# Top-k attention and a SmeLU MLP: transposes of the unit matrix in TensorE's program until the MLP's first products

## The chip, the cores and the metric

The kernel runs on one core of a Trainium2 chip. The metric is the device time of one execution in microseconds (us), of which the median over several executions is compared. Five engines work side by side: TensorE (PE; its weight loads are shown apart as PEld), VectorE (DVE), ScalarE (ACT), GpSimd (POOL) and SyncE (SP), which issues the transfers. Each runs its own list of instructions in order and waits for the others at semaphores.

## What is computed

```python
# q, k, v: (8 batches, 8 heads, 576 rows, 64); float32 throughout
scores = q @ k.T / sqrt(64)
kth    = 32nd largest score of each row
attn   = softmax(where(scores >= kth, scores, -1e9))
x      = (attn @ v), heads side by side        # (4608, 512)
h      = x @ w_in                              # (4608, 2048)
g      = where(h >= 1, h, where(h <= -1, 0, (h + 1)**2 / 4))
out    = g @ w_out                             # (4608, 512)
```

## The kernel before, in words

**Steps.** A step is one block of 128 query rows for a pair of heads. `rounds` lists (batch, block t), and each block has four head pairs (`hp`), so that the first four steps, m = 0 to 3, are block 0 of batch 0. In a step TensorE makes the scores (`sp`, L354), ACT scales them into `s` (L355), DVE finds the 32nd largest with MAX8 and MATCH_REPLACE8 (L368 to L447) and masks the exponentials `e` (L454), which ACT made (L391). Then the masked weights are turned: in the early steps by TensorE, as a product with a diagonal matrix that also divides by the row sum (`diag` on ACT, L404; `pw`, L469, and `pwt`, L475; copied by ACT to `wT`, L472 and L476). TensorE multiplies them with the values (`po`, L502), and ACT copies the result to `xT` (L515). When four head pairs of a block are there, `mlp` puts the block's products (`ph`, L535, and `py`, L558) into the list `pending`.

**The order of work.** Inside `run` the order of PE, DVE, ACT and POOL is the program's (`tc.manual_schedule`); SP's is the scheduler's. The loop over m has seven places (`SLOTS`) per step. Each place issues a part of DVE's search for step m, and certain places issue the rest: place 1 turns the weights of step m - 1 (`transpose_w`), place 2 multiplies those by the values (`values_until`), place 4 makes the scores of step m + 2 (`begin_at`), place 6 the queries of step m + 3. In the first steps (`early`) the 32 pieces of the two weight matrices are converted as well, four to a step, with ACT (L146, L147), DVE (L155) and POOL (L157). At the end of a place `advance` takes products from `pending` as far as a budget allows; `spent` counts what has been taken. `pending` is empty until `values_until` has done step 3, which is in place 2 of m = 4.

**Before the loop.** Once, while the first keys are being loaded, TensorE transposes the unit matrix 20 times (`warm`, L672). `ident` is 128x128 float32, made by POOL. Then come keys (`pk`, `pkt`), queries (`pq`) and the scores of steps 0 and 1.

**PSUM** holds 8 banks: tag `a` two buffers of two banks (`sp`, `pw`, `pwt`, `pk`, `pq`), tag `ph` three of one bank (`ph`, `po`), and tag `py` one bank, first used by the MLP's second product.

Of the kernel before, what the change touches and what calls it, by code (L numbers as in the profile page):

```python
# [11 lines left out]
F32 = mybir.dt.float32  # L12
# [14 lines left out]
def kernel(  # L27
# [10 lines left out]
    nc = tc.nc  # L38
# [3 lines left out]
    P = 128  # L42
# [4 lines left out]
    NT = S // P  # L47
# [13 lines left out]
    ident = const.tile([P, P], F32, name="ident")  # L61
# [64 lines left out]
    def load(pool, i, bufs=3, parts=1):  # L126
        if i < n_pieces * parts and i not in loaded:
            if room:
                loaded[i] = room[i % len(room)]
            else:  # L130
                loaded[i] = pool.tile([P, 2 * WC // parts], U32, name="raw", bufs=min(bufs, 2))
            c = i % parts * (WC // parts)
            nc.sync.dma_start(out=loaded[i], in_=pieces_of_weights[i // parts][1][:, c:c + WC // parts].bitcast(U32))
# [42 lines left out]
    def run(ctx, paired):  # L176
# [5 lines left out]
        ps = ctx.enter_context(tc.tile_pool(name="ps", bufs=1, space=PSUM))  # L182
# [103 lines left out]
        def finish_turns():  # L286
            while turns:
                turns.pop(0)()
# [174 lines left out]
        def transpose_w(st):  # L463
            w = st["e"]
            st["wT"] = wT = (late or words).tile([P, BLOCKS, P], F32, name="wT", bufs=4 if late else 1)
            pt = ps.tile([P, 2, NT, P], F32, name="pw", tag="a", bufs=2)
            for i in range(2):
                for c in range(NT):
                    nc.tensor.matmul(pt[:, i, c, :], w[:, i, main(i)][:, c * P:(c + 1) * P], st["rz"][:, i, :],  # L469
                                     start=True, stop=True)  # L470
            for i in range(2):
                nc.scalar.copy(wT[:, i * (NT + 1):i * (NT + 1) + NT], pt[:, i])  # L472
            pt = ps.tile([P, P], F32, name="pwt", tag="a", bufs=2)
            for i in range(2):
                nc.tensor.matmul(pt[i * TL:(i + 1) * TL, :], w[:, i, tail(i)], st["rz"][:, i, :], start=True, stop=True)  # L475
            nc.scalar.copy(wT[:, NT], pt)  # L476
# [123 lines left out]
        pending = deque()  # L600
        total, spent = len(chunks) * (NK * NF + NF * DM // P), 0
# [4 lines left out]
        def convert(time):  # L606

            nonlocal converted, begun
            while begun < min(converted + (2 if paired else 1), n_pieces):
                pipe.append(convert_piece(words, begun, not paired))  # L610
                next(pipe[-1])
                begun += 1
            next(pipe.popleft())
            converted += 1
            usable[converted] = time
            for i in range(begun, converted + (len(room) or 2)):
                load(words, i)

        def inspect():
            nonlocal inspected  # L620
            if paired and inspected < 2 * n_pieces:
                inspect_piece(late, inspected)
                inspected += 1
# [7 lines left out]
        def take():  # L631

            nonlocal spent, due, pe_time, taken
            cost, pieces, work, _ = pending[0]
            if pieces > converted or usable[pieces] > pe_time + 0.5:
                return False
            pending.popleft()
            due -= cost
            spent += cost
            pe_time += cost * UNIT_TIME  # L640
            work()
            taken = work.func
            return True

        def advance(amount, until):

            nonlocal due, pe_time
            due = due + amount if pending else 0.0
            pe_time = max(pe_time, until - 4.0)
            while pending and due >= pending[0][0] and pe_time < until and take():  # L650
                pass
            due = min(due, 24.0)
# [84 lines left out]
        for m in range(n + 2):  # L737
            early = converted < n_pieces
            if not early and first_late is None:
                first_late = m  # L740
            elif not early and late is None:
                conversion.close()
                room.clear()
                late = ctx.enter_context(tc.tile_pool(name="late", bufs=1))

            share, left = (total - spent) / (n + 2 - m), sum(x[0] for x in pending)
            for r in sorted(ready):
                if r + 4 > m and r >= valued:
                    share = min(share, left / (r + 4 - m))
                    left += NK * NF + NF * DM // P  # L750
            top_k, parts = None, [0] * SLOTS
            if m < n:
                top_k = weights(state[m], state[m - 1] if m > 0 else None, state[m + 1] if m + 1 < n else None)
                parts = [1] * SLOTS if early else [1, 1, 0, 1, 1, 1, 1]
                start = max(dve_time, scored[m])
                now_converting = range(0, SLOTS, 2)
                dve_time = start + K_TIME + PIECE_TIME * min(len(now_converting), n_pieces - converted)
                done[m] = dve_time
                state[m]["by_tensor"] = early or m >= n - 2
            for slot in range(SLOTS):  # L760
                now = start + (dve_time - start) * (slot + 1) / SLOTS
                for _ in range(parts[slot]):
                    next(top_k, None)
                if m < n and converted < n_pieces:
                    if slot in now_converting:
                        convert(now)
                elif slot == 3 and late is not None:
                    if m % 2:
                        inspect()
                    elif paired:  # L770
                        load(late, inspected, 1, 2)
                if slot == 1 and 1 <= m <= n and state[m - 1]["by_tensor"]:
                    pe_time = max(pe_time, done[m - 1] + 2.0) + 1.0
                    transpose_w(state[m - 1])
                    ready_at[m - 1] = pe_time + 1.8
                if slot == 3 and 1 <= m <= n and state[m - 1] is not None and not state[m - 1]["by_tensor"]:
                    move_w(state[m - 1])
                    ready_at[m - 1] = done[m - 1] + 15.0
                if slot == 3:
                    finish_turns()  # L780
                if slot == 2 and m == n and paired:
                    judge(ps, att)
                if slot == 2 and (early or m == first_late or m >= n - 1):
                    values_until(m)
                if m == 0 and slot in (1, 2):
                    next(first)
                if slot == 2 and not early:
                    if m % 2 == 0:
                        while pending and taken is not None and taken.__name__ == "hidden" and take():
                            pass  # L790
                    values_until((m - 2) // 2 * 2)
                if slot == (4 if early else 2):
                    begin_at(m + 2)
                if slot == (6 if early else 1):
                    queries(m + 3)
                    if (m < n and prep is None and next_keys < B and steps[m][0] == next_keys - 1 and steps[m][1] >= 1
                            and (next_keys > 1 or converted == n_pieces)):
                        prep = (turned_keys_of if next_keys > 1 else keys_of)(next_keys)
                    if prep is not None and (m % 2 == 0 or next_keys == 1):
                        got = next(prep, None)  # L800
                        pe_time += 0.5 if next_keys < 2 else 0.0
                        if got is None:
                            prep, next_keys = None, next_keys + 1
                        else:
                            keys[next_keys] = got
                            value_loads = got.get("loads", value_loads)
                    elif value_loads is not None:
                        next(value_loads, None)
                advance((EARLY_SHARE if early else share) / SLOTS if m < n else 32.0, now)
            for _ in (top_k if top_k is not None else ()):  # L810
                pass
# [17 lines left out]
    with ExitStack() as inner:  # L829
        run(inner, True)  # L830
# [31 lines left out]
```

## Time and profile before

| | us |
|---|---|
| median of 3 runs | 1506.48 |
| the three runs | 1506.18, 1506.48, 1512.55 |
| profiled execution, its own time | 1507.81 |
| its span, first to last instruction | 1506.0 |
| PE busy in the span | 1441.7 |
| DVE busy | 1411.9 |
| ACT busy | 1158.4 |
| POOL busy | 908.5 |

The page of the profile gives sums; what one stage costs is read from the timeline (instructions in order, with the idle time ahead of them and what ended it in brackets), from the list of waits, and from windows (busy time of each engine in a stretch, with the clock that TensorE was granted: 1.00 is full speed, 0.50 half). All times inside an execution are counted from the start of its span. The stretch that the change bears on ends some 76 us into it, where the MLP's first products stand.

### The profile page before, as it was taken

What the parts mean: (1) busy time and instruction counts of PE and PEld (TensorE: products, weight loads), DVE (VectorE), ACT (ScalarE), POOL (GpSimd) and SP (SyncE); (2) the same over time, 40 slices, a digit from 0 to 9 for tenths busy, and PEclk for the clock granted to TensorE, in tenths of its full rate; (3) what the DMA queues carried; (4) which work ended last, traced back from release to release, by engine and by line L of the source; (5) the groups of instructions that cost most, each with busy time, mean ns of one, the idle gap of its engine ahead of it and who ended that gap; (6) DMA issues with size and microseconds to landing.
All of it is one profiled execution on the core that took longest, in us unless ns stands there. A gap on an engine that the chain in (4) does not pass through costs nothing.

```text
span 1506.0 us, 31908 instructions
## 1 busy us (share of the span) xinstructions
PE 1441.7 (96%) x10605; PEld 1034.8 (69%) x10605; DVE 1411.9 (94%) x4392; ACT 1158.4 (77%) x2221; POOL 908.5 (60%) x1309
## 2 busy tenths in 40 slices
PE   5698899999999999999999999999999999999998
PEld 3476577677777777677777777767777777777675
DVE  6989999999999999999999999999999999999912
ACT  6887788877778888687778888788778887877732
POOL 3463566666666666556666666666666666666630
PEclk6799899999999999999999999999999999999999
DMA  8632667785667787886677796787667877655510
GB/s 255 199 116 86 158 165 185 196 196 152 172 189 200 201 189 185 211 197 182 164 197 186 202 199 184 200 219 183 165 192 186 203 183 183 163 156 144 142 32 17
DMA packets 510318, 260.93 MB, mean 173 GB/s; under 512 B 460992, under 2 KB 469184, under 8 KB 510144
## 3 DMA queue, kind: packets, MB, share of 16 engines
q1 hardware_dynamic: 510144, 258.80, 66.3%
q8 instruction: 86, 1.41, 0.4%
q14 instruction: 88, 0.72, 0.1%
HBM read 62.91 MB, written 102.63 MB: 110 GB/s over the span
## 4 chain that ended last, share of the span: by engine, by line
PE 66%; DVE 20%; ACT 6%; DMA 3%; issue 3%; POOL 1%; SPq 1%; ACTq 0%; POOLq 0%
PE ph L535 24%; PE py L558 24%; PE sp L354 8%; PE po L502 8%; DVE more L375 5%; DVE e L454 4%; DVE less L368 2%; DVE more L368 2%; DMA rows<-halves 2%; PE pw L469 2%; DVE tops L416 2%; DVE tops L424 2%; DVE tops L435 2%; DVE seconds L442 2%; DVE tops L388 1%
## 5 line engine op out<-in xcount | busy, mean ns | idle before, releaser
L535 PEld LDWEIGHTS ph<-xT,w_in 128*128 128x128 f32 x4608 | 548.5, 193 | 100.0 <-issue 78.6
L535 PE MATMUL ph<-xT,w_in 128*128 128x128 f32 x4608 | 558.0, 277 | 1.3 <-ACT g L546 0.7
L558 PE MATMUL py<-w_out,g 128*128 128x512 f32 x1152 | 556.4, 603 | 1.7 <-ACT y L561 1.7
L551 POOL TENSOR_SCALAR r<-r 128x256 f32<-128x256 f32 x276 | 146.8, 532 | 453.6 <-ACT r L539 453.4
L375 DVE MATCH_REPLACE8 more<-tops,more 128x288 f32<-128x288 f32 x864 | 374.9, 437 | 0.0
L558 PEld LDWEIGHTS py<-w_out,g 128*128 128x128 f32 x1152 | 195.2, 190 | 166.9 <-issue 158.6
L484 ACT COPY halves<-e 128x1152 uint16<-128x1152 uint16 x268 | 293.6, 1143 | 13.4 <-DMA rows<-halves 13.4
L454 DVE SCALAR_TENSOR_TENSOR e<-s,kth,e 128x577 f32<-128x577 f32 x288 | 259.6, 937 | 0.8 <-ACT e L391 0.6
L553 POOL TENSOR_TENSOR g<-r,g 128x256 f32<-128x256 f32 x280 | 240.9, 860 | 22.0
L407 POOL TENSOR_SCALAR e<-e,rz 128x576 f32<-128x576 f32 x268 | 223.4, 843 | 12.6 <-DVE rz L400 12.6
L391 ACT ACTIVATE e<-s,nmax 128x576 f32<-128x576 f32 x288 | 222.5, 773 | 4.7
L539 ACT ACTIVATE r<-ph,half 128x256 f32<-128x256 f32 (+1 forms) x296 | 135.7, 458 | 116.4 <-PE ph L535 92.3
L355 ACT ACTIVATE s<-sp 128x576 f32<-128x576 f32 x288 | 171.9, 648 | 57.3 <-PE sp L354 55.6
L552 POOL TENSOR_TENSOR r<-r 128x256 f32<-128x256 f32 x276 | 190.1, 689 | 23.0
L354 PE MATMUL sp<-kT,qT 64*128 64x288 f32 x1024 | 164.1, 437 | 10.6 <-ACT kT L257 8.4
L502 PEld LDWEIGHTS po<-wT,v_in 128*64 128x64 f32 x2048 | 116.0, 139 | 60.5 <-ACT g L546 47.3
L502 PE MATMUL po<-wT,v_in 128*64 128x128 f32 x2048 | 142.1, 280 | 10.0 <-ACT g L546 6.5
L354 PEld LDWEIGHTS sp<-kT,qT 64*128 64x128 f32 x1024 | 89.7, 189 | 73.6 <-ACT r L539 28.0
L368 DVE TENSOR_TENSOR more<-s 128x576 f32<-128x576 f32 x144 | 112.3, 780 | 19.9 <-ACT s L355 19.9
L546 ACT ACTIVATE g<-ph,minus 128x256 f32<-128x256 f32 x280 | 129.8, 464 | 0.0
L416 DVE MAX8 tops<-more 128x8 f32<-128x288 f32 x288 | 125.4, 442 | 0.0
L368 DVE TENSOR_TENSOR less<-s 128x576 f32<-128x576 f32 x144 | 122.4, 850 | 0.0
(88 smaller groups left out, 1349.4 us busy)
## 6 DMA issues: line engine op xcount, KB each, us to landing
rows<-halves SPq DMA_DIRECT2D x134, 576.0 KB, 3.0
lines<-parts SPq DMA_DIRECT2D x48, 256.0 KB, 2.9
q_in<-in_q_dram SPq DMA_DIRECT2D x32, 256.0 KB, 3.7
v_in<-in_v_dram SPq DMA_DIRECT2D x32, 256.0 KB, 4.1
out_dram<-y SPq DMA_DIRECT2D x32, 256.0 KB, 2.8
raw<-in_moe_w_in_dram SPq DMA_DIRECT2D x32, 256.0 KB, 3.2
raw<-in_moe_w_out_dram SPq DMA_DIRECT2D x32, 256.0 KB, 3.3
kT<-in_moe_w_in_dram SPq DMA_DIRECT2D x8, 512.0 KB, 4.8
```

The costliest lines, as they stand in the source:

```text
L354: nc.tensor.matmul(*x, start=True, stop=True)
L368: nc.vector.tensor_tensor(out=x, in0=s[:, :, 0:SH], in1=s[:, :, SH:S], op=op)
L375: nc.vector.match_replace(out=st["rest"][:, i, :], in_to_replace=eight(st["tops"], i, r - 8), in_values=src[:, i, :], imm_value=LOWEST)
L391: nc.scalar.activation(e[:, i, :], s[:, i, :], AF.Exp, bias=nmax[:, i:i + 1])
L407: nc.gpsimd.tensor_scalar(st["e"][:, i, :], st["e"][:, i, :], rz[:, i:i + 1], 1.0, ALU.mult, ALU.mult)
L454: nc.vector.scalar_tensor_tensor(out=st["all"][1][:, i, :], in0=st["all"][0][:, i, :], scalar=last[i], in1=st["all"][1][:, i, :], op0=ALU. ...
L484: nc.scalar.copy(halves[:, :, i * S:(i + 1) * S], st["e"][:, i, :].bitcast(U16).rearrange("p (k t) -> p t k", t=2))
L502: nc.tensor.matmul(po[j * D:(j + 1) * D], v_in[:, h, c, :] if c < NT else v_tl[0][:, h, :], wT[:, block(j, c)], start=(c == 0), stop=(c == ...
L535: nc.tensor.matmul(ph[:, i], w_in[:, kk, f * P:(f + 1) * P], xT[:, kk], start=(kk == 0), stop=(kk == NK - 1))
L552: nc.gpsimd.tensor_tensor(out=r, in0=r, in1=r, op=ALU.mult)
L553: nc.gpsimd.tensor_tensor(out=g, in0=r, in1=g, op=ALU.add)
L558: nc.tensor.matmul(py[0], gs[f // group][:, f % group], w_out[:, f, :], start=(f == 0), stop=(f == NF - 1))
```

## The change

In each place, while no product of the MLP has been taken and none is pending, five transposes of the unit matrix are issued on TensorE into a tile of tag `py`. Nothing reads it.

```diff
                     elif value_loads is not None:
                         next(value_loads, None)
+                if paired and early and spent == 0 and not pending:
+                    rest = ps.tile([P, NT, P], F32, name="rest", tag="py", bufs=1)
+                    for i in range(5):
+                        nc.tensor.transpose(rest[:, i % NT, :], ident, ident)
                 advance((EARLY_SHARE if early else share) / SLOTS if m < n else 32.0, now)
```

In TensorE's order this makes 30 groups of five, 150 transposes: four steps of seven places, and places 0 and 1 of m = 4. Between the work that was there they stand so:

```
m = 0: sp(step 1), 5, pk, 5, pk, 10, sp(step 2), 20, pw(step 0)
m = 1: pw, pwt, 5, po, 10, sp(step 3), 10, pq, 10, pw(step 1)
m = 2: pw, pwt, 5, po, 10, sp(step 4), 20, pw(step 2)
m = 3: pw, pwt, 5, po, 10, sp(step 5), 20, pw(step 3)
m = 4: pw, pwt, 5, po, then the MLP's first products
```

Each group has a new tile in the one buffer of the tag, and from the second group on its first transpose carries a wait for TensorE's own semaphore. The orders of DVE, ACT and POOL are unchanged. On SP five small loads of batch 1's value tails (`v_tail`, L197 and L202) shift by up to five places among the loads of weight pieces (L133).

## The prediction

> **What bounds the kernel now.** I read the page first: it says where the whole span goes, and in which slices TensorE's clock is low.
>
> ```profile
> span 1506.0 us, 31908 instructions
> ...
> PE 1441.7 (96%) x10605; PEld 1034.8 (69%) x10605; DVE 1411.9 (94%) x4392; ACT 1158.4 (77%) x2221; POOL 908.5 (60%) x1309
> ...
> PEclk6799899999999999999999999999999999999999
> ```
>
> PE and DVE are both almost full, but the first two or three slices (37.65 us each) stand apart: that is where the clock digits are low. The change lies wholly in them, so its worth is read there. The windows answer, cut at the times where the granted clock may change, gives the mechanism (columns: stretch, its length, busy time of PE, PEld, DVE, ACT, POOL, then clock, DMA share and GB/s):
>
> ```profile
> 18.82:22.24 3.42, 3.26 (x13) 1.76 (x9) 3.42 (x12) 2.76 (x5) 1.27 (x1) 0.50 1.13 316
> ...
> 29.06:32.47 3.41, 0.12 (x1) 0.12 (x1) 3.41 (x10) 3.35 (x7) 2.28 (x4) 0.50 0.86 254
> 32.47:35.89 3.42, 3.42 (x16) 3.37 (x16) 3.42 (x7) 1.55 (x3) 0.94 (x2) 0.50 0.70 238
> 35.89:39.30 3.41, 3.05 (x32) 2.14 (x32) 3.41 (x12) 3.12 (x7) 1.26 (x1) 1.00 0.66 187
> 39.30:42.71 3.41, 0.59 (x6) 0.18 (x3) 3.41 (x14) 3.38 (x7) 1.98 (x2) 1.00 0.81 232
> ```
>
> The clock moves in stretches of 3.41 us. A stretch full of PE work (32.47 to 35.89) is followed by the full clock; one that is 0.59 of 3.41 us busy is followed by the half clock at 42.71. A stretch that is 3.26 busy, partly with the 64-row score products, is not followed by a rise. Meanwhile DVE is 3.41 of 3.41 busy and ACT nearly so: this stage belongs to them. Next, what do they wait for? The list of waits between 20 and 76 us (who waited, for whom: us in all, times, longest):
>
> ```profile
> ACT wT L472 <- PE pw L469: 8.2, 4, 2.1
> ...
> DVE more L368 <- ACT s L355: 2.6, 2, 1.3
> ```
>
> Four times ACT stands 2.1 us at the turned weights, and twice that reaches DVE. The timeline of PE shows why the product is slow, and when it is not:
>
> ```profile
> 64.13 1.24 PE L354 MATMUL sp<-kT,qT 64*128 64x288 f32 x8
> 70.16 3.60 PE L469 MATMUL pw<-diag,e 128*128 128x128 f32 x16 [4.78 <-ACT diag L404]
> ...
> 87.69 2.05 PE L469 MATMUL pw<-diag,e 128*128 128x128 f32 x16 [0.16 <-ACT diag L404]
> ```
>
> Sixteen `pw` take 3.60 us after 4.78 us idle, and 2.05 us with the clock up. The other three early ones took 3.73, 3.78 and 3.78 (timeline, at 32.35, 45.26, 57.70). The chain of waits puts these four, and ACT's work between them, on the path that sets the end; the DVE timeline adds a third gap, at the fifth step:
>
> ```profile
> 82.42 0.94 DVE L368 TENSOR_TENSOR more<-s 128x576 f32<-128x576 f32 x1 [2.81 <-ACT s L355]
> ```
>
> **The change part by part.** It removes nothing, and adds 150 transposes.
>
> *Do they raise the clock?* The nearest row is the 20 `warm` transposes of the same matrix at the start, as its answer by source line has it (ns: least, median, most):
>
> ```profile
> L672 PE MATMUL warm<-ident x20: 272/421/473, 2.0 to 5.7; 128*128 128x128 f32 x20
> ```
>
> They alone ran on TensorE from 2.01 us; the clock's first recorded rise is at 5.17, and the last ones take 272 ns instead of 421. So they count as work. The Trainium skill, "TensorE: Matmul & The Clock Gate", Part 4 (PE-mode transpose), speaks against this: it says transposes don't bring the gate to full rate, as they don't count as busy. By that rule the change would be the slower rival below; by the row it is not, and the row decides. That page's Part 1 gives an activity window of about 3.4 us, which the stretches above show as 3.41.
>
> *Price of a group of five.* From `pk`, four transposes at full clock take 0.60 us (at 5.76), at half clock 1.11 (at 12.54); from `pw`, 16 take 2.05 and 3.74, so one more is (2.05 - 0.60)/12 = 0.12 us, or 0.22 at half clock. If a group follows on without a gap, it costs 5 x 0.12 = 0.60 (1.10). If its first waits until the last of the group before has ended, 0.60 + 0.12 = 0.72 (1.33). No row shows such a wait of TensorE for its own last instruction, so these are the two ends, with some 0.1 more for the semaphore. I take 0.72 and 1.33, since the wait is in the program.
>
> *Where they stand, clock up.* From one `pw` to the next: `pw` 2.05; `pwt` and five transposes about 1.2, of which ACT's copies to `wT` (1.07 + 0.28) cover nearly all; `po` 1.7; ten 1.44; `sp` 1.24; twenty 2.88. Sum 10.5 us. Before, it was 57.70 - 45.26 = 12.44. DVE's own step is 55.98 - 43.76 - 1.28 = 10.94. So at full clock they fit under DVE; the cover is only 0.4 us per step, and without it PE itself would set the step.
>
> *Where they stand, clock down.* In m = 0 the clock is at half. `sp` of step 1 ends at 20.06; five (1.1) push the first `pk` by 1.1 to 1.4 us, five more the second by some 2.5. ACT copies the first at 22.08 (`pk` then ends at about 22.3: 0.3 late) and the second at 25.93 (not late). The stretch 22.24 to 25.65 is then transposes with two short gaps, roughly 3.0 of 3.41 us. Between the 3.26 that raised nothing (half-array products in it) and the fuller ones that did, I take it as enough, at two to one: the clock comes up at 25.65, and the twenty ahead of the first `pw` end by 28.2 + 2.9 = 31.1, before `diag` frees `pw` at 32.35.
>
> *What it saves.* Each early `pw` falls from about 3.73 to 2.05, so ACT waits 0.4 instead of 2.1: 4 x 1.7 = 6.8 us less on ACT. DVE caps this: it gets back only its gaps, 1.28 + 1.32 + 2.81 = 5.4 us. What is late next is DVE itself. Less 0.3 to 0.4 for the late `pk`: **5.0 us**.
>
> *Does it last?* After 76 us every engine starts from there, in the same order, and from 200 to 400 us DVE is 200.0 of 200 us busy and PE 197.8: what is done earlier there ends earlier. I carry it in full; 0 is the other end. Beyond it, the clock drops again from 138 to 142 and 155 to 166 us in before; a shift of 5 us cuts those stretches differently, and one stretch at half clock is 3.41/2 = 1.7 us of PE work, either way, up to about three of them.
>
> *Other edits.* The bank of `py` lies idle until the MLP: 0. The moved SP loads belong to batch 1 and are used long after; the weight loads they change places with have ACT's 2 us stalls as cover. If a weight piece came late by the four small loads it would cost their 2.55 us of issue (timeline, 47.41); I take 0.
>
> **Sum.** The profiled execution took 1507.8; 1507.8 - 5.0 = 1502.8. It stands 1.3 above the median of 1506.5, so I put the median after at **1501.5**.
>
> **The rivals.**
> *B, the clock comes up too late for the first `pw`.* The twenty then run at half clock: 29.2 + 4 x 1.33 = 34.5 at least, and `pw`, at 3.74, ends 2.2 to 2.4 late. It raises the clock itself (as in before), and the other three stalls shrink by 1.7 each: 2.4 - 5.1 = -2.7, or 1503.8. For it: gaps between groups, and 3.26 that raised nothing.
> *C, slower: the transposes hold no clock, and TensorE becomes the bound by them.* Every rise then comes from `pw` itself and lasts 6.83 us (35.89 to 42.71). After it: 1.2 + 1.7 + 1.44 + 1.24 leaves about 1.2 us at full clock for the twenty; the remaining 12 or so take 3.2, and the next `pw` is 0.8 to 1.4 us late where it has 8.7 us (49.04 to 57.70). With 2.4 in m = 0 that is +5 to +6.5, or 1511.5 to 1513; twice that if the clock falls one stretch earlier. It decides where twenty transposes outlast the 4.8 us that PE idles ahead of `pw`, thus at 0.24 us each or more. Against it: the rise at 5.17, and no fall at 8.58, after a stretch that was 2.24 busy with little but transposes.
> *D, the early microseconds don't last.* From 76 to 100 us PE is 22.25 of 24 us busy; if that stage has its own pace, or the drops at 138 to 166 us take the gain back, nothing is left: 1506.5. Against it: the products there wait for nothing that has a fixed time.
>
> **How the numbers follow.** A 0.50, B 0.22, D 0.14, C 0.14. A's own range is 1498 to 1504 (full DVE gaps and one favourable stretch; groups with 0.1 more). The range reaches to D and leaves out C and A's best tail: 1497.5 to 1510. Half a per cent is 7.5 us, about what a measurement of this kernel can tell from no change. Below 1499.0 lies only A's tail: 0.12. Above 1514.0 lies C's worse half: 0.05. Between: 0.83.
>
> **What would show it.** A: clock 1.00 from about 26 to 76 us; four `pw` of 2.05; ACT's wait for them some 0.4 each; DVE without its gaps at 56, 68 and 82 us. B: the same from 39 us on, the first `pw` near 34.5 and 3.7 long. C: the clock falling between `pw` as before, PE without idle time ahead of `pw`, and ACT waiting longer than 2.1 there. D: DVE's fifth `more` near 77 us, yet the end within 1 us. I am wrong if a group costs over 0.85 us at full clock, for then PE's step passes DVE's, or if the early part is 5 us shorter and a later stretch of low clock eats or doubles it.

## The result, and the profile after

Over 20 runs of each the median is 1505.39 us with the change (1499.31 to 1510.03) and 1511.35 before (1506.18 to 1515.45). The ratio is 0.9959, with a 95% interval of 0.9949 to 0.9969: 6.2 us less, between 4.7 and 7.7 (the two medians themselves differ by 5.96). Of the three runs that the prediction had of the kernel before, two are the fastest of its 20, and their median was one of them. The mean granted clock of a whole execution was 0.984 to 0.992 in the 20 runs with the change, and 0.973 to 0.982 in the 33 runs of the kernel before that stand beside the first experiments: the change raises it in every run, not only in the profiled one.

The page of the kernel after, the same three lines:

```profile
span 1503.0 us, 32202 instructions
...
PE 1451.9 (97%) x10755; PEld 1043.6 (69%) x10755; DVE 1413.6 (94%) x4392; ACT 1159.2 (77%) x2221; POOL 905.5 (60%) x1309
...
PEclk8999999999999999999999999999999999999999
```

PE is busy 10 us longer, though the span is 3 us shorter: the transposes are work, but work in time that PE stood idle. The low clock digits of the first slices are gone. ACT's timeline after, at the four copies that wait for `pw` (the bracket is the idle time ahead and what ended it):

```profile
35.02 1.07 ACT L472 COPY wT<-pw 128x512 f32<-128x512 f32 x2 [0.37 <-PE pw L469]
...
46.33 1.08 ACT L472 COPY wT<-pw 128x512 f32<-128x512 f32 x2 [0.35 <-PE pw L469]
...
57.13 1.07 ACT L472 COPY wT<-pw 128x512 f32<-128x512 f32 x2 [0.35 <-PE pw L469]
...
68.20 1.07 ACT L472 COPY wT<-pw 128x512 f32<-128x512 f32 x2 [0.36 <-PE pw L469]
```

Four waits of 0.36 us where there were 8.2 us in four. PE's timeline after, from the twenty transposes of m = 0 on:

```profile
28.41 4.67 PE L812 MATMUL rest<-ident 128*128 128x128 f32 x20
32.94 2.05 PE L469 MATMUL pw<-diag,e 128*128 128x128 f32 x16
...
50.22 1.24 PE L354 MATMUL sp<-kT,qT 64*128 64x288 f32 x8
51.39 3.23 PE L812 MATMUL rest<-ident 128*128 128x128 f32 x20
55.05 2.05 PE L469 MATMUL pw<-diag,e 128*128 128x128 f32 x16 [0.42 <-ACT diag L404]
...
82.50 2.05 PE L469 MATMUL pw<-diag,e 128*128 128x128 f32 x16 [0.17 <-ACT diag L404]
```

Each `pw` takes 2.05 us. The fifth stands at 82.50, and stood at 87.69; the profiled execution after began its loop 0.56 us later (`sp` of step 1 at 17.61, before at 17.05), so the stretch from there to the fifth `pw` is 5.8 us shorter. DVE's timeline after has no gap of its own in the three places where it had 5.4 us:

```profile
56.23 0.89 DVE L368 TENSOR_TENSOR more<-s 128x576 f32<-128x576 f32 x1
...
67.55 0.74 DVE L368 TENSOR_TENSOR more<-s 128x576 f32<-128x576 f32 x1
...
78.12 0.74 DVE L368 TENSOR_TENSOR more<-s 128x576 f32<-128x576 f32 x1
...
87.81 0.62 DVE L155 TENSOR_SCALAR bits<-kT 128x512 uint32<-128x512 uint32 x1 [1.18 <-POOL w_out L157]
...
93.84 1.85 DVE L368 TENSOR_TENSOR more<-s 128x576 f32<-128x576 f32 x1 [0.86 <-ACT s L355]
```

Its next wait is one for POOL, which it had before too (1.17 us at 92.31). The last of these rows is `more` of one step on; before, it read:

```profile
99.01 1.86 DVE L368 TENSOR_TENSOR more<-s 128x576 f32<-128x576 f32 x1 [1.53 <-ACT s L355]
```

**Where the profiled pair loses some of it.** Its spans differ by 3.0 us, not by 5.8. The starts of `more` tell where: 6.2 us earlier than before at 928, 3.5 from 1028 on (times of the kernel before). In between, in the window from 955 to 1000 us, ACT's waits for the transfer `rows` are 5.4 us before and 7.8 after. In the profile of an experiment below (e7_sooner) they are 2.1, and an earlier stage, at 620 to 660 us, differs between profiles by some 4 us too. The granted clock differs there with them: in the windows 600 to 660 and 940 to 1010 us it is 0.97 and 0.98 before, 0.97 and 0.95 after, and 1.00 in both in e7. Whether the slower clock makes these stages late or follows from their waits is not shown; medians are needed to see through them.

### The profile page after: what moved, and what is told of

It is laid out like the page before. It is cut to its first block, busy times and chain, and to the rows that moved or that the text cites. A ratio compares the mean times of both kernels' runs of the same rounds, so it can differ in the third digit from the quotient of the medians.

```text
span 1503.0 us, 32202 instructions
## 1 busy us (share of the span) xinstructions
PE 1451.9 (97%) x10755; PEld 1043.6 (69%) x10755; DVE 1413.6 (94%) x4392; ACT 1159.2 (77%) x2221; POOL 905.5 (60%) x1309
## 3 DMA queue, kind: packets, MB, share of 16 engines
q8 instruction: 87, 1.43, 0.4%
## 4 chain that ended last, share of the span: by engine, by line
PE 85%; DVE 6%; ACT 4%; DMA 2%; issue 2%; POOL 0%; SPq 0%; ACTq 0%; POOLq 0%
PE ph L535 31%; PE py L558 31%; PE sp L354 10%; PE po L502 9%; DVE more L375 1%; PE po L510 1%; DMA rows<-halves 1%; PE pw L469 1%; DVE e L454 1%; DMA wT<-rows 1%; DVE more L368 1%; ACT halves L484 1%; ACT e L391 1%; ACT units L146 1%; DVE tops L416 0%
## 5 line engine op out<-in xcount | busy, mean ns | idle before, releaser
L551 POOL TENSOR_SCALAR r<-r 128x256 f32<-128x256 f32 x276 | 142.9, 518 | 453.9 <-ACT r L539 453.8
```

## The experiments

The ratios are to the kernel before, with 95% intervals (6 to 20 runs of each kernel; the last column is from one profile of each, but for e6).

| kernel | transposes | ratio | interval | ACT's waits for pw, 20 to 76 us |
|---|---|---|---|---|
| before | 0 | 1 | | 8.2 |
| the change | 150 | 0.9959 | 0.9949 to 0.9969 | 1.4 |
| e1_one | 30 | 1.0 | 0.9988 to 1.0012 | 8.2 |
| e2_m0 | 35 | 0.9997 | 0.9983 to 1.0011 | 7.6 |
| e3_ten | 300 | 1.0015 | 1.0004 to 1.0027 | 8.4 (to 78 us) |
| e4_onetile | 150 | 0.9962 | 0.9951 to 0.9974 | 3.1 |
| e5_ahead | 85 | 0.9983 | 0.9972 to 0.9994 | 3.4 |
| e6_behind | 65 | 0.9979 | 0.9963 to 0.9996 | 7.2, 7.0, 7.2 (three profiles) |
| e7_sooner | 180 | 0.9954 | 0.9937 to 0.9970 | 1.4 |

**One transpose per place** (e1_one).

```diff
-                    for i in range(5):
+                    for i in range(1):
```

> One transpose in each place instead of five (30 in all); SyncE's order is that of the changed kernel. Theory (the gain is TensorE's clock at the four early pw): one transpose is 0.1 to 0.3 us per place and leaves PE idle nearly as long as before, so the clock falls as before, the early pw stay at 3.6 to 3.8 us, ACT waits about 2 us at each, ratio to the kernel before 0.999 to 1.001. Rival (the gain is the moved transfers or any filler at all): 0.996 as with five.

As the theory had it: the ratio is 1.0. The order of SP is that of the change, so the moved transfers are worth nothing, and neither is a transpose as such. The list of waits of this kernel, 20 to 76 us, has before's two rows unchanged:

```profile
ACT wT L472 <- PE pw L469: 8.2, 4, 2.1
DVE more L368 <- ACT s L355: 2.6, 2, 1.3
```

**In step 0 alone** (e2_m0).

```diff
-                if paired and early and spent == 0 and not pending:
+                if paired and m == 0 and spent == 0 and not pending:
```

> Five transposes per place in step m = 0 only (35 in all). Theory (each step pays for its own cold pw): the first pw is 2.05 us and its wait 0.4, the three others stay near 3.7 and 2.1; ACT is 1.7 us earlier, DVE's gaps shrink from 5.4 to some 3.7 us; ratio 0.9989. Rival (one rise of the clock at the start is all that counts): 0.996.

The rival falls: a clock that has come up once does not give the gain (0.9997). The theory's 0.9989 lies in the interval, but its first `pw` was expected at 2.05 us. PE's timeline has it at 3.27:

```profile
27.73 2.41 PE L812 MATMUL rest<-ident 128*128 128x128 f32 x15
32.25 3.27 PE L469 MATMUL pw<-diag,e 128*128 128x128 f32 x16 [2.10 <-ACT diag L404]
```

Here the five of place 0 of m = 1 are missing, so fifteen stand ahead of `pw`, they end 2.1 us before it, and the clock falls once more, at 32.85: the stretch from 29.43 was 1.32 of 3.42 us busy. So what stands just ahead of `pw` counts.

**Ten per place** (e3_ten).

```diff
-                    for i in range(5):
+                    for i in range(10):
```

> Ten transposes per place instead of five (300 in all). Theory (five still lie under DVE's step; TensorE has 0.4 us per step to spare with them): doubling adds 35 x 0.155 = 5.4 us to each step less 0.4, so PE sets the step at about 16 us where it was 12.4 before; with 3 to 5 us more in m = 0 it ends 12 to 16 us above the kernel before, ratio 1.008 to 1.010, and ACT waits for sp. Rival (they run only where TensorE idles anyway): 0.996.

Slower, as expected, by far less: 2.3 us (0.6 to 4.1) instead of 12 to 16. The mechanism is in PE's timeline, where this step has no idle time left:

```profile
48.04 1.95 PE L469 MATMUL pw<-diag,e 128*128 128x128 f32 x16
49.92 0.44 PE L475 MATMUL pwt<-diag,e 128*64 128x128 f32 x4
50.29 1.31 PE L812 MATMUL rest<-ident 128*128 128x128 f32 x10
51.53 1.09 PE L502 MATMUL po<-wT,v_in 128*64 128x128 f32 x16
52.46 0.39 PE L502 MATMUL po<-wT,v_tail 128*64 128x128 f32 x4
52.77 2.68 PE L812 MATMUL rest<-ident 128*128 128x128 f32 x20
55.39 1.24 PE L354 MATMUL sp<-kT,qT 64*128 64x288 f32 x8
56.56 5.42 PE L812 MATMUL rest<-ident 128*128 128x128 f32 x40
```

The next `pw` starts at 61.82: a step of 13.8 us, set by PE, where 16 was expected. The price was wrong: 0.155 us per transpose holds the wait between groups, and there are still 30 groups; the bare transpose is 0.12. That is 35 x 0.12 = 4.2 us, less 0.4 idle time and, as an estimate, some 0.6 that ACT's copies to `wT` cover. Three steps then add 3 x 1.4 = 4 us to the 12.4 us of before, not 11, and the first `pw` starts 1.8 us later (34.11 for 32.35). The profile is 5.2 us behind at 111 us; the median shows less than half of that, and where the rest goes is open. ACT waits up to 2.9 us for `pw` again, now not for a slow one but for a late one.

**One tile for all groups** (e4_onetile).

```diff
-        first_late = None
+        first_late, rest = None, None
 ...
-                    rest = ps.tile([P, NT, P], F32, name="rest", tag="py", bufs=1)
+                    rest = rest if rest is not None else ps.tile([P, NT, P], F32, name="rest", tag="py", bufs=1)
```

> The same 150 transposes into one tile for all groups, so that no group waits for the one before it. Theory (the wait costs 0.2 us per group, but PE has time to spare): twenty take 2.4 to 2.5 us at full clock instead of 3.23; the time is that of the changed kernel, ratio 0.995 to 0.997. Rival (the groups delay pw, sp or pk, and part of the gain is lost to that): faster than the changed kernel by 1 us or more, 0.995 or below.

As expected, 0.9962. Twenty take 2.40 us instead of 3.23, so the wait is worth 0.2 us per group, which PE has to spare. One thing was not expected, in PE's timeline:

```profile
28.44 0.76 PE L354 MATMUL sp<-kT,qT 64*128 64x288 f32 x4 [2.11 <-ACT kT L257]
29.13 2.40 PE L812 MATMUL rest<-ident 128*128 128x128 f32 x20
33.69 2.65 PE L469 MATMUL pw<-diag,e 128*128 128x128 f32 x11 [2.15 <-ACT diag L404]
```

(The window cuts off the last five `pw`; all 16 take 3.68 us.) Cheaper filler ends earlier, and the first `pw` is slow again, with 2.01 us of waiting. The other three come after 1.0 to 1.5 us idle and stay at 2.05. Here the stretch ahead of the slow one (30.37 to 33.79) was 1.27 us busy, and the one with the 1.52 us gap (54.27 to 57.68) 1.89. DVE passes on a part: it waits 1.02 us at 78.92 and 1.10 at 108.65, where the change has no wait, and by 111 us it is 3.8 us ahead of before (2.5, with a loop that began 1.3 us later) where the change is 5.7. The second wait follows another fall of the clock, at 98.64, after PE had idled 2.06 us ahead of the sixth `pw`; the change has this gap too, 2.07 us, and there the clock held. The median does not show the difference; its interval is 1.8 us to either side, and the phase of the stretches (when they begin, against the program) need not be that of this profile in the other runs.

**Only ahead of pw, and only behind it** (e5_ahead, e6_behind).

```diff
-                if paired and early and spent == 0 and not pending:
+                if paired and early and slot in (0, 4, 5, 6) and spent == 0 and not pending:
```

> The groups of places 4, 5, 6 and 0 alone (85 transposes, nearly all in the stretch between sp and pw; none between pwt, po and sp). Theory (what counts is that PE does not idle for most of a 3.41 us stretch ahead of pw): pw of steps 1 to 3 take 2.05 us with waits of 0.4; in m = 0 the twenty may run at half clock and make the first pw up to 1.5 us late. Ratio 0.996 to 0.9975. Rival (the clock needs PE filled all through the step): pw near 3.7, ratio 0.999 to 1.

By the medians more than half the gain is lost (0.9983). The ratio lies between the two expectations, and its interval touches both, so the profile has to tell. It gives neither: the first two `pw` are fast, as in the theory, the others 3.63 and 2.46 us. Windows of this kernel around the third (columns as before; the clock falls at 55.48):

```profile
51.90:55.30 3.40, 1.42 (x11) 0.94 (x11) 3.40 (x12) 3.37 (x7) 2.90 (x3) 1.00 0.59 144
55.30:58.70 3.40, 3.40 (x16) 3.33 (x16) 3.40 (x11) 1.69 (x3) 1.27 (x1) 0.53 0.91 356
```

Without the fifteen between `pwt` and `sp` the twenty start and end 1.5 us earlier; PE then idles 1.92 us ahead of `pw`, and the stretch before it is less than half busy. So in this execution the groups behind `pw` are needed as well, to push the twenty up against the next one. That accounts for only a part of what the median loses, though: at 111 us this profile is 4.5 us ahead of before, counted with its later loop, where the change is 5.7 and e4 3.8, and yet e4 has the better median. What else sets the medians apart is open.

```diff
-                if paired and early and spent == 0 and not pending:
+                if paired and early and slot in (1, 2, 3) and spent == 0 and not pending:
```

> The groups of places 1, 2 and 3 alone (65 transposes, between pwt, po and sp; none ahead of pw). Theory: PE idles 3 to 5 us ahead of each pw as before, the clock falls there or has just fallen, pw take 3.2 to 3.8 us, waits near 2; ratio 0.9985 to 1.000. Rival (any 65 transposes give their share of the gain): 0.998 or below, waits near 1.2.

The ratio, 0.9979, came out below what the theory expected and where the rival had it, though its interval reaches the theory too, while the profile shows waits of 1.4 to 2.1 us. Two more profiles of the same kernel bear on this.

> A second profile of the kernel with the groups of places 1 to 3 alone, whose median came out 0.2 per cent below the kernel before while its first profile shows no gain at 112 us. Theory (its pw lie at the edge of a stretch, so the phase of the 3.41 us stretches against the program decides from run to run): the start of the stretches differs, and some of the four waits for pw are 0.4 to 1.2 us instead of 1.4 to 2.1; DVE is then 1 to 4 us ahead at 112 us. Rival (the start gains nothing in any run; its lower median comes from later stages that vary): waits of 1.4 to 2.1 again.

> A third profile of the same kernel, with the same expectations as the second.

Waits sum to 7.2, 7.0 and 7.2 us in the three, and in each another one or two of the four `pw` are shorter (3.07 and 3.42; 2.71; 2.65). Which one is shorter differs between executions of the same kernel, as the theory of the phase has it, and in the second and third one wait of four is 1.0 us; but the sum stays. At 111 us DVE is 0.9 and 0.7 us ahead of before in the second and third, 0.9 behind in the first (0.6 ahead at 99 us). That is less than the theory's 1 to 4 us; the upper end of the interval, 0.9996, would be 0.6 us. What else there is in the median is open; the granted clock of the other runs of this kernel was up to 0.985, that of the three profiled ones 0.978, 0.982 and 0.983.

**Sooner, too** (e7_sooner).

```diff
         begin_at(0)
+        rest_of(10)
 ...
         next(first)
+        rest_of(20)
         begin_at(1)
```

(`rest_of` issues that many transposes of the unit matrix into a tile of tag `py`.)

> The change, and before the loop ten transposes more ahead of the second pk and twenty ahead of the scores of step 1, which fills PE's idle time from 10.5 to 17 us. Theory (DVE is the cap: it has no gap between 17.6 and 87 us with the change): sp of step 1 falls from 3.0 to about 1.3 us and ACT's wait for it from 2.1 to some 1.0, yet the end stays that of the change, ratio 0.995 to 0.9965. Rival (every cold product of the start is on the path): 1.2 us faster than the change, 0.995 or below.

As expected, the ratio is that of the change (0.9954; the intervals overlap, and this one leaves room for the rival too). ACT's wait for the scores of step 1 falls from 2.14 to 1.56 us only, for `sp` still caught the falling clock (2.09 us, not 1.3). DVE's starts of `more` are within 0.2 us of the change's up to 158 us: the 0.6 us that ACT gains there, DVE does not pass on. Its profiled span, 1497.2, is shorter than that of the change mostly by way of the two later stages: counted by `more`, it is 0.6 us ahead of the change at 601 us, 3.4 from 711 on and 6.4 from 1024 on (times of the change). `more` at the first of them, in the kernel before, the change and this one, on DVE's timelines:

```profile
638.68 0.98 DVE L368 TENSOR_TENSOR more<-s 128x576 f32<-128x576 f32 x1 [2.71 <-ACT s L355]
```

```profile
632.44 0.98 DVE L368 TENSOR_TENSOR more<-s 128x576 f32<-128x576 f32 x1 [2.73 <-ACT s L355]
```

```profile
629.03 0.82 DVE L368 TENSOR_TENSOR more<-s 128x576 f32<-128x576 f32 x1 [0.43 <-ACT s L355]
```

No kernel tried is shown to be faster than the change.

## Why the prediction was right

*Transposes raise the clock: right.* In the kernel after, PE runs nothing but transposes of the unit matrix from 29.31 to 32.72 us, and the clock rises at the end of it (the third number from the right is the clock):

```profile
29.31:32.72 3.41, 3.29 (x14) 2.49 (x15) 3.41 (x11) 3.35 (x6) 2.27 (x3) 0.50 0.88 232
32.72:36.13 3.41, 3.41 (x29) 2.86 (x28) 3.41 (x8) 3.01 (x7) 1.27 (x1) 1.00 0.81 292
```

The rule in the Trainium skill, "TensorE: Matmul & The Clock Gate", Part 4 (PE-mode transpose), that transposes do not count as busy, does not hold for these float32 ones.

*The price of a group: a little low.* The sum took 0.72 us and named 0.1 more without counting it; measured 3.23/4 = 0.81. The other end, 0.60 without the wait, is e4's 2.40/4.

*They fit under DVE's step, barely: right.* A step of PE was put at 10.5 us; it is 55.05 - 44.24 = 10.8 with 0.42 idle. e3 shows what follows when they no longer fit.

*Step 0: the outcome right, the way there not.* The clock was to come up at 25.65 and stay. It came up at 22.48, fell at 29.31, since PE had idled 2.01 us ahead of the second half of `sp` (a stretch 1.53 of 3.41 us busy), and rose at 32.72, just in time for `pw` at 32.94. The two stretches that end with the first rise and with the fall:

```profile
19.07:22.48 3.41, 3.41 (x15) 2.50 (x12) 3.41 (x14) 2.44 (x4) 1.27 (x1) 0.50 1.09 323
...
25.90:29.31 3.41, 1.53 (x10) 0.91 (x11) 3.41 (x13) 3.32 (x6) 0.67 (x1) 1.00 1.04 243
```

The twenty, at half clock in part, took 4.67 us and not 2.9, which used up all of PE's slack. That the rise met `pw` so closely was luck: in e5 and e7 it did so again, in e2 and e4 the filler ran at full clock and ended early, the clock fell just as `pw` began (at 32.85 and 33.79), and `pw` was slow.

*ACT saves 6.8, DVE caps it at 5.4: right.* 8.2 - 1.4 = 6.8, and DVE's three gaps are gone. By the `more` at 78.12 (82.42 before) DVE is 4.3 us earlier, 4.9 with the later loop: the 5.0 of the forecast. One step on it is 5.7, for there its wait fell from 1.53 to 0.86 us, which the prediction did not have. e7 shows that 0.6 us more on ACT are not passed on.

*It lasts: right in the median.* 5.0 was forecast and 6.2 measured; the forecast lies inside the interval of 4.7 to 7.7. From 157 to 607 us of the profiled pair `more` is 5.4 to 7.2 us earlier throughout. The 1.2 us between forecast and measurement are not attributed; the shorter wait one step on, 0.7 us in the profiled pair, may be a part.

*The median itself*, 1501.5, was 3.9 too low, because the median of three runs that it was counted from was 4.9 below that of 20. By itself 1505.4 lies above the 1498 to 1504 that the prediction gave its own mechanism, and nearer to rival D's 1506.5; it is the ratio to the kernel before, and the profile, that speak for the mechanism.

*The rivals.* B's outcome, a slow first `pw` and three fast ones, did not come with the change but with e4, and there in another way: the clock was not late, it fell again. Of C, transposes that hold no clock did not show; PE as the bound came with ten per place, at full clock. D, a later stage that takes a part of the gain back, is seen in the profiled pair, and not in the medians.

## What to carry to other kernels

Filler on an idle TensorE is worth just the slow products that something on the path waits for; find those waits first, and see which engine caps the gain next. Place it by where it ends: keep the gap just ahead of the product short. With the clock up, 1.0 to 1.5 us held here (e4); with 1.9 to 2.2 it fell in e2, e4 and e5, and held with 2.07 ahead of the sixth `pw` of the change, so that it depends on where the stretches of 3.41 us begin. Work earlier in the step helps by pushing the filler towards it. Count its own time against the engine's slack, bare work and waits between groups apart.

## What the runs showed of the hardware that was not expected

The clock fell after stretches of 3.41 us in which TensorE was 1.3 to 1.5 us busy, while PE was idle for only 1.9 to 2.2 us at a time (1.27 in e4, to 33.79; 1.43 in e5, to 55.48; 1.53 in the change, to 29.31). No sharp bound shows: it fell after one of 1.83 in e1 (39.22 to 42.63, more than half of it the 64-row products `sp`), and in the change it held after this one, with a gap of 2.07 us, so that the sixth `pw` took 2.05 us:

```profile
94.16:97.58 3.42, 1.54 (x13) 1.54 (x14) 3.42 (x5) 3.36 (x7) 3.34 (x3) 1.00 0.70 240
97.58:100.99 3.41, 3.05 (x33) 2.27 (x32) 3.41 (x13) 2.99 (x8) 1.26 (x1) 1.00 0.72 243
```

Where the stretches begin differs between executions, so the same program can meet a fall or not. A TensorE instruction that waits for TensorE's own last one costs 0.2 us per group of five here (3.23 against 2.40 us for twenty).
